# One key block of every three gets its distance factor as the bias of the exponential, and the lists of small work around the attention are re-sorted

## The chip, the cores and the metric

The kernel runs on one core of a Trainium2 chip. The metric is the device time of one execution in microseconds (us). A run of the chip is timed several times and the median is given; one further execution is taken by the hardware profiler, and all durations below come from that one.

## The reference, cut to what matters

Attention over 8 batches, 8 heads, 576 positions and 64 channels, with a window of 128 keys and a penalty that grows with the distance between query and key, is followed by a layer of 8 experts in which every token goes to the one expert with the highest gate.

```python
scores = (1 / np.sqrt(D)) * np.matmul(q, k.transpose(0, 1, 3, 2))
rel = pos[:, None] - pos[None, :]
slopes = 2.0 ** (-8.0 * (np.arange(H) + 1) / H)
mask = (rel >= 0) & (rel < 128)
scores = np.where(mask, scores - slopes * np.abs(rel), -1e9)      # per head
attn = softmax(scores);  x = (attn @ v) as rows of 512            # 4608 tokens
logits = x @ w_gate;  expert = argmax(logits)
y = gate_weight * (relu(x @ w1[expert]) @ w2[expert])             # w1 512x1024, w2 1024x512
```

All of it is float32. A factor that depends on the query alone falls out of the softmax, since it stands above and below the fraction.

## The kernel before, in words

**Attention.** The work is cut into 16 units: 4 pairs of batches (`bp`) times 4 pairs of heads (`hp`). Keys and queries come in 9 blocks of 64 positions (`KB`). A key block meets the queries of its own block and of the next two: block distance 0, where the later keys are masked, 1, where every key is seen, and 2, where the keys that are too old are masked. A unit has four groups `g`: key blocks 0-1, 2-3, 4-5 and 6-8. For a group, `scores(i)` issues 8 or 12 matmuls into a PSUM tile `sp` (two buffers), ScalarE takes the exponential of all 768 columns (L775) into `pe` (six buffers), and VectorE multiplies all 768 columns with the factor `fac`, which holds exp(-slope * distance), zero where masked (L778, L783). `values` multiplies `pe` with the values into the PSUM tile `at` (one buffer of two banks, L804), `finish` copies `at` to `xT` on ScalarE (L821, L823) and sums `pe` over the keys by matmuls (L836); VectorE adds these to `sumT` (L847).

The order of all instructions is written out by hand: the loop runs over `i`, the number of the group, and scores are issued three groups ahead of the values that need them. SyncE loads keys, queries and values two units ahead.

**Small work behind the attention.** When a pair of batches is done, `behind(bp)` hands out a list of small steps, one entry popped by `some()` per group: `gate` (gate logits, matmul and L861), `turn`, `scale_a` to `scale_c` (softmax denominators, argmax; `es` at L952), `count`, `place` (the token's slot in its expert's list), `ones_at` and `enlist` (the lists of token numbers by matmul), and the writing of the token rows to a DRAM tensor `x_rows`. For `bp` 0 the rows are turned on VectorE (`squares_turned`, L1091, into four buffers `xs`), get their scale on POOL (L1099, after `scales_squared` L1073) and leave by POOL's queue, four DMAs for each tile of 128 tokens (`squares_out`, L1108). For `bp` 1 and 2 they are turned on TensorE (L1044) and copied by ScalarE (L1046). The last entry of `bp` 2 is `early_table` and `gather(fixed[0])`: POOL fetches the first 4 x 128 tokens of expert 0 by indirect DMA (L1240).

**Experts.** A group of 512 tokens is gathered, scaled on VectorE (`to_scale`, L1252), turned into columns (`to_columns`: TensorE L1265 and ScalarE L1266 for experts 0 and 1, VectorE L1268 for the others), and multiplied by both weight matrices with seven instead of eight block products: `strassen1` (L1454) and `strassen2` (L1511), fourteen steps each. After each step, `step()` pops one entry of the list `fill`. The small work of the last pair of batches (`with_tail`) fills the 14 steps of expert 0's `strassen1`; the tables of all experts (`table_fixed`, `count_all`, `check_all`, `table_further`, `pieces` L1142), the gather of expert 1 and its preparation fill expert 0's `strassen2`. Before `strassen1`, everything left in `tasks` is issued at once: expert 0's last columns and sums.

## Time and profile before

| | us |
|---|---|
| median of 3 runs (684.91 to 687.83) | 686.86 |
| the profiled execution | 691.06 |
| its span, first to last instruction | 689.2 |
| TensorE matmul busy in the span | 655.8 |
| VectorE / ScalarE / POOL busy in the span | 379.4 / 199.2 / 237.6 |
| unit 1's first value matmul starts at | 21.3 |
| expert 0's first product starts at | 180.7 |
| expert 1's first product starts at | 244.8 |

In the views, PE is TensorE's matmuls, PEld its weight loads, DVE VectorE, ACT ScalarE, SP SyncE; L and a number is a line of the kernel. A group of instructions is shown as engine, operation, output<-inputs, shapes and count, then its busy time and the mean of one. "PEclk" is the granted share of TensorE's clock.

### The profile page before, as it was taken

The page shows a single profiled execution, that of the slowest core. Times are in us where ns is not written, and L with a number is a line of the kernel's source. Part 1 is how long each engine was busy: PE and PEld are TensorE (multiplying, and loading weights), DVE is VectorE, ACT ScalarE, POOL GpSimd, SP SyncE. Part 2 cuts the span into 40 slices and gives each one's busy share as a digit, 9 for nine tenths or more (in the row PEclk, how much of TensorE's full clock was granted, in tenths as well). Part 3 has the DMA queues.
Part 4 walks back from the last instruction along what each step waited for, and adds up shares of the span by engine and source line. Part 5 has one row for each costly group of instructions (what it writes and reads, how often), then busy time and mean ns, then how long its engine had stood idle before and what let it go on. Part 6 is the DMA issues. An engine that isn't in the chain of part 4 may idle for free.

```text
span 689.2 us, 14460 instructions
## 1 busy us (share of the span) xinstructions
PE 655.8 (95%) x6004; PEld 548.2 (80%) x6004; DVE 379.4 (55%) x717; ACT 199.2 (29%) x365; POOL 237.6 (34%) x360
## 2 busy tenths in 40 slices
PE   5899889998999899999999999999999999999996
PEld 4778768687687788878897887888788978878893
DVE  4567769786489476614842564275148435633500
ACT  5555446465331223113202310231131123002210
POOL 8100572215001176117323702652172247023020
PEclk9999899999999999999999999999999999999999
DMA  9677987854516964185448237652844573284010
GB/s 285 200 222 192 287 241 219 289 157 149 165 22 162 386 206 140 57 292 170 155 154 301 57 129 258 212 166 63 296 137 145 178 276 97 86 305 154 1 62 8
DMA packets 63549, 122.00 MB, mean 177 GB/s; under 512 B 5905, under 2 KB 30001, under 8 KB 63474
## 3 DMA queue, kind: packets, MB, share of 16 engines
q1 hardware_dynamic: 51778, 92.78, 42.0%
q0 software_dynamic: 10544, 27.31, 12.4%
q8 instruction: 49, 0.80, 0.5%
q10 hardware_dynamic: 1152, 0.88, 0.4%
q14 instruction: 26, 0.21, 0.1%
HBM read 101.79 MB, written 19.96 MB: 177 GB/s over the span
## 4 chain that ended last, share of the span: by engine, by line
PE 75%; issue 9%; DVE 8%; DMA 4%; POOL 2%; ACT 1%; SPq 0%; POOLq 0%; DVEq 0%; ACTq 0%
PE sp L769 5%; PE at L804 5%; PE pair0b L1511 4%; PE pair0a L1511 4%; PE pair0b L1454 4%; PE pair0a L1454 4%; PE pair1a L1511 4%; PE pair1b L1511 4%; PE pair2b L1454 4%; PE pair1b L1454 4%; PE pair1a L1454 4%; PE pair2a L1454 4%; PE pair2a L1511 4%; PE pair2b L1511 4%; PE m L836 3%
## 5 line engine op out<-in xcount | busy, mean ns | idle before, releaser
L1240 POOL DMA_INDIRECT xg<-x_rows,p_idx x124 | 125.0, 1008 | 37.8 <-issue 37.5
L1534 POOL DMA_INDIRECT out_dram<-zo,s_idx x39 | 44.5, 1140 | 250.6 <-DVE zo L1525 149.6
L769 PE MATMUL sp<-q_sb,k_sb 64*64 64x192 f32 (+2 forms) x1152 | 60.2, 331 | 7.1 <-DMA q_sb<-in_qT_dram 6.9
L775 ACT ACTIVATE pe<-sp 128x768 f32<-128x768 f32 x64 | 51.9, 811 | 49.6 <-PE sp L769 46.7
L804 PE MATMUL at<-pe,v_sb 64*64 64x192 f32 (+2 forms) x1408 | 59.6, 289 | 3.4 <-issue 3.4
L778 DVE TENSOR_TENSOR pe<-pe,fac 128x768 f32<-128x768 f32 x48 | 45.5, 952 | 28.3 <-ACT pe L775 27.8
L804 PEld LDWEIGHTS at<-pe,v_sb 64*64 64x64 f32 x1408 | 48.0, 138 | 9.5 <-issue 6.9
L769 PEld LDWEIGHTS sp<-q_sb,k_sb 64*64 64x64 f32 x1152 | 42.0, 141 | 16.6 <-DMA q_sb<-in_qT_dram 4.3
L1465 ACT ACTIVATE h<-h 128x512 f32<-128x512 f32 x32 | 20.2, 631 | 41.3 <-DVE h L1464 41.3
L836 PE MATMUL m<-pe,ind 128*32 128x192 f32 (+2 forms) x704 | 29.8, 288 | 0.6 <-issue 0.6
L1252 DVE TENSOR_TENSOR xn<-xg 128x512 f32<-128x512 f32 x39 | 26.3, 676 | 3.4 <-DMA xg<-x_rows,g_idx 3.1
L836 PEld LDWEIGHTS m<-pe,ind 128*32 128x32 f32 x704 | 23.2, 110 | 3.0 <-issue 1.0
L1108 POOL DMA_DIRECT2D x_rows<-xs x40 | 21.6, 548 | 6.4 <-POOL xs L1099 1.9
L783 DVE TENSOR_TENSOR pe<-pe,fac 128x768 f32<-128x768 f32 x16 | 15.3, 955 | 15.2 <-ACT pe L775 15.1
L1268 DVE STREAM_TRANSPOSE xgT<-xn 128x512 f32<-128x512 f32 x31 | 22.1, 712 | 1.1
L538 DVE TENSOR_TENSOR w2s<-w 128x512 f32<-128x512 f32 x16 | 10.9, 684 | 19.4 <-DMA w<-in_moe_w_dram 19.4
L1099 POOL COPY xs<-sq 128x16 f32<-128x16 f32 x10 | 2.6, 258 | 53.8 <-ACT sq L1081 53.8
L1566 PE MATMUL pair2a<-w,h 128*128 128x512 f32 x48 | 21.1, 592 | 0.0
L821 ACT COPY xT<-at 128x640 f32<-128x640 f32 (+1 forms) x32 | 18.7, 585 | 6.5 <-PE at L804 4.6
L1454 PE MATMUL pair0b<-xgT,w 128*128 128x256 f32 x72 | 17.2, 382 | 0.0
L1511 PE MATMUL pair1a<-w,h 128*128 128x256 f32 x72 | 17.0, 379 | 0.0
L1454 PE MATMUL pair0a<-xgT,w 128*128 128x256 f32 x72 | 17.0, 379 | 0.0
(375 smaller groups left out, 1393.2 us busy)
## 6 DMA issues: line engine op xcount, KB each, us to landing
w<-in_moe_w_dram SPq DMA_DIRECT2D x29, 2048.0 KB, 7.9
k_sb<-in_kT_dram SPq DMA_DIRECT2D x15, 576.0 KB, 5.6
q_sb<-in_qT_dram SPq DMA_DIRECT2D x15, 576.0 KB, 5.6
v_sb<-in_v_dram SPq DMA_DIRECT2D x30, 288.0 KB, 4.5
x_rows<-xs POOLq DMA_DIRECT2D x16, 264.0 KB, 3.8
x_rows<-xs POOLq DMA_DIRECT2D x32, 66.0 KB, 4.7
x_rows<-xT SPq DMA_DIRECT2D x8, 264.0 KB, 5.2
w<-in_moe_w_dram SPq DMA_DIRECT2D x4, 512.0 KB, 7.7
```

What stands on the lines that cost most here:

```text
L769: nc.tensor.matmul(sp[c * KB : (c + 1) * KB, r, c0 : c0 + n], lhsT=k_sb[u][hs, c, kb * KB : (kb + 1) * KB], rhs=q_sb[u][hs, c, kb * KB : k ...
L775: nc.scalar.activation(pe[:], sp[:, :, :GC], AF.Exp, scale=SCALE)
L778: nc.vector.tensor_tensor(pe.rearrange("p r (k c) -> p r k c", k=2), pe.rearrange("p r (k c) -> p r k c", k=2), fac[:, h0 : h0 + 2, None, ...
L804: nc.tensor.matmul(acc[r * D : (r + 1) * D, c, lo - q0 : hi - q0], lhsT=v_sb[u][c * KB : (c + 1) * KB, kb, r * D : (r + 1) * D], rhs=pe[c ...
L836: nc.tensor.matmul(sm[32 * j : 32 * j + 32, lo - q0 : hi - q0], lhsT=none[:] if pe is None else ind[:, hp, :], rhs=fac[:, 0, :KB] if pe is ...
L1108: eng.dma_start(x_d[r0 : r0 + n * m, a * PW : (a + 1) * PW].rearrange("(k i) w -> i k w", i=TQ), xs[a * TQ : (a + 1) * TQ, p0 // TQ : p0 / ...
L1240: nc.gpsimd.indirect_dma_start(out=to, out_offset=None, in_=where, in_offset=bass.IndirectOffsetOnAxis(ap=idx, axis=0),)
L1252: nc.vector.tensor_tensor(xn[:], x, s.unsqueeze(3).to_broadcast([P, NA, HP, TQ]), op=ALU.mult)
L1268: nc.vector.transpose(to.rearrange("p h (k j) -> p k h j", j=TQ), xn[:])
L1454: nc.tensor.matmul(ps[:, f * 256 : (f + 1) * 256], lhsT=left[m][:, d, fb * P : (fb + 1) * P], rhs=right[m][:, d, :], start=(m in (1, 2, 5) ...
L1511: nc.tensor.matmul(ps[:, :256], lhsT=left[m][:, f, c * P : (c + 1) * P], rhs=right[m][:, f, :], start=(m in (1, 2, 5) and f == 0), stop=Tr ...
L1534: ins = nc.gpsimd.indirect_dma_start(out=out[:, :], out_offset=bass.IndirectOffsetOnAxis(ap=s_idx[:, g["c0"] + j : g["c0"] + j + 1], axis= ...
```

## The change

1. **The exponential and the factor.** Within a group the columns are sorted by block distance: of the three stretches of 128 columns, the first holds distance 0, the second distance 1, the third distance 2 (in the last group, the diagonal block of key block 8 takes a free place in the third). The factor of the query is dropped, since it cancels. What is left of the factor for distance 1 depends on the key alone, that is on the partition: it goes into the exponential as its bias, `mid`, a column of 128 values for each head. So the exponential of a group is three instructions instead of one, 128x512 (distances 0 and 2, both heads) and two of 128x128 with a bias; VectorE multiplies 512 columns instead of 768. The matmuls are as many and as large as before; their moving operand and their output now have up to three stretches of 64 columns. The constants are made in other steps (`seen_i`, `rel_i`, `mid_i`, `far`).
2. **Scores ahead.** In units 0 and 1 the scores are issued two groups ahead, from unit 2 on three as before.
3. **Lists.** `bp` 2: `early_table` is cut in two, the first half (`early_holes`) moves up to the last row writing, the rest and the gather move up by one entry, into the one of `enlist`. The preparation of expert 0 begins one group later, and only its first three entries stay ahead of `strassen1`; the last two of its four column steps and its sums go into the first two steps of `strassen1`. `with_tail` is spread anew: `ones_at`, `enlist` and `end_of_tail` (which loads expert 1's weights) move to `strassen2`'s first six steps, all sums of w2 come into `strassen1`; the eight small row DMAs of the last tile move from SyncE's queue to POOL's. In `strassen2` the tables follow from step 6, expert 1's first two column steps are in steps 11 and 12, and the last two with half of its weight sums and its other sums go into expert 1's `strassen1`.

The diff, cut to its core:

```diff
@@ -641,27 +639,44 @@
-PIECES = ((0, 192), (192, 128), (320, 64))
+seen_i = ac.tile([P, GC], I32, name="seen_i")
 rel_i = ac.tile([P, GC], I32, name="rel_i")
+mid_i = ac.tile([P, 1], I32, name="mid_i")
+NEAR = (0, 1, 4)
 for b in range(2):
-    for c0, n in PIECES:
+    half = slice(b * KB, (b + 1) * KB)
+    nc.gpsimd.iota(seen_i[half, : 5 * KB], pattern=[[0, 5], [1, KB]], base=0, channel_multiplier=-1)
+    for c0, n, e in ((0, 2, 32), (2, 2, 160), (4, 1, 32)):
         nc.gpsimd.iota(
-            rel_i[b * KB : (b + 1) * KB, c0 : c0 + n], pattern=[[1, n]], base=0, channel_multiplier=-1,
-        )
+            rel_i[half, c0 * KB : (c0 + n) * KB], pattern=[[0, n * KB]], base=e, channel_multiplier=-1,
+        )
+    nc.gpsimd.iota(mid_i[half, :], pattern=[[0, 1]], base=-96, channel_multiplier=1)
+seen = ep.tile([P, 2, GC], F32, name="pe")
+far = seen[:, 1, :]
+nc.vector.tensor_copy(seen[:, 0, : 5 * KB], seen_i[:, : 5 * KB])
 rel = ac.tile([P, GC], F32, name="rel")
-nc.vector.tensor_copy(rel[:], rel_i[:])
-far = ep.tile([P, 2, GC], F32, name="pe")
-nc.vector.tensor_scalar(far[:, 0, :], rel[:], scalar1=0.0, scalar2=BIG, op0=ALU.is_lt, op1=ALU.mult)
-nc.vector.tensor_scalar(far[:, 1, :], rel[:], scalar1=127.5, scalar2=BIG, op0=ALU.is_ge, op1=ALU.mult)
-nc.vector.scalar_tensor_tensor(
-    rel[:], in0=rel[:], scalar=0.0, in1=far[:, 0, :], op0=ALU.max, op1=ALU.add,
-)
-nc.vector.tensor_add(rel[:], rel[:], far[:, 1, :])
+nc.vector.tensor_copy(rel[:, : 5 * KB], rel_i[:, : 5 * KB])
+for c0, n, op in ((0, 2, ALU.is_lt), (2, 2, ALU.is_ge), (4, 1, ALU.is_lt)):
+    cs = slice(c0 * KB, (c0 + n) * KB)
+    nc.vector.tensor_scalar(far[:, cs], seen[:, 0, cs], scalar1=0.0, scalar2=BIG, op0=op, op1=ALU.mult)
+nc.vector.tensor_add(rel[:, : 5 * KB], rel[:, : 5 * KB], far[:, : 5 * KB])
 fac = ac.tile([P, H, GC], F32, name="fac")
+mid = ac.tile([P, H], F32, name="mid")
+mid_p = ac.tile([P, 1], F32, name="mid_p")
+nc.vector.tensor_copy(mid_p[:], mid_i[:])
+for h in range(H):
+    nc.vector.tensor_scalar(
+        mid[:, h : h + 1], mid_p[:], scalar1=2.0 ** (-8.0 * (h + 1) / H), scalar2=None, op0=ALU.mult,
+    )
 def factors(hp):
     for h in (2 * hp, 2 * hp + 1):
-        nc.scalar.activation(fac[:, h, :], rel[:], AF.Exp, scale=-(2.0 ** (-8.0 * (h + 1) / H)))
+        nc.scalar.activation(
+            fac[:, h, : 5 * KB], rel[:, : 5 * KB], AF.Exp, scale=-(2.0 ** (-8.0 * (h + 1) / H)),
+        )
 factors(0)
@@ -762,32 +777,40 @@
     sp = ps_s.tile([P, 2, 512], F32, name="sp")
-    for kb, c0, n in GR[g]:
+    for kb in range(2 * g, 2 * g + 2) if g < 3 else range(6, 9):
+        n = min(3, NK - kb)
         for c in range(2):
...
                 nc.tensor.matmul(
-                    sp[c * KB : (c + 1) * KB, r, c0 : c0 + n],
+                    by_distance(sp[c * KB : (c + 1) * KB, r, :GC], kb, 0, n),
                     lhsT=k_sb[u][hs, c, kb * KB : (kb + 1) * KB],
-                    rhs=q_sb[u][hs, c, kb * KB : kb * KB + n], start=True, stop=True,
+                    rhs=q_sb[u][hs, c, kb * KB : (kb + n) * KB].rearrange("p (j x) -> p j x", x=KB),
+                    start=True, stop=True,
                 )
     pe = ep.tile([P, 2, GC], F32, name="pe")
-    nc.scalar.activation(pe[:], sp[:, :, :GC], AF.Exp, scale=SCALE)
     h0 = 2 * units[u][1]
-    if g < 3:
-        nc.vector.tensor_tensor(
-            pe.rearrange("p r (k c) -> p r k c", k=2), pe.rearrange("p r (k c) -> p r k c", k=2),
-            fac[:, h0 : h0 + 2, None, :192].to_broadcast([P, 2, 2, 192]), op=ALU.mult,
-        )
-    else:
-        nc.vector.tensor_tensor(pe[:], pe[:], fac[:, h0 : h0 + 2, :], op=ALU.mult)
+    outer = pe.rearrange("p r (j x) -> p r j x", j=3)[:, :, 0:3:2, :]
+    nc.scalar.activation(
+        outer, sp[:, :, :GC].rearrange("p r (j x) -> p r j x", j=3)[:, :, 0:3:2, :], AF.Exp, scale=SCALE,
+    )
+    w = 2 * KB if g < 3 else 3 * KB
+    nc.vector.tensor_tensor(
+        outer, outer,
+        fac[:, h0 : h0 + 2, : 2 * w].rearrange("p r (j x) -> p r j x", j=2)[:, :, :, : 2 * KB], op=ALU.mult,
+    )
+    for r in range(2):
+        inner = slice(2 * KB, 4 * KB)
+        nc.scalar.activation(
+            pe[:, r, inner], sp[:, r, inner], AF.Exp, bias=mid[:, h0 + r : h0 + r + 1], scale=SCALE,
+        )
     prob[i] = pe
-def block(u, kb):
-    g = min(kb // 2, 3)
-    c0, n = next((c, n) for k, c, n in GR[g] if k == kb)
-    return prob[4 * u + g], c0, n
+def by_distance(x, kb, a, b):
+    if kb == NK - 1:
+        return x[:, 5 * KB :].rearrange("p (j x) -> p j x", j=1)
+    return x.rearrange("p (j k x) -> p j k x", j=3, k=2)[:, a:b, kb % 2, :]
 def values(u, half, kbs):
@@ -797,14 +820,15 @@
     for kb in kbs:
-        pe, c0, n = block(u, kb)
-        lo, hi = max(q0, kb * KB), min(q0 + qn, kb * KB + n)
+        pe = prob[4 * u + min(kb // 2, 3)]
+        lo, hi = max(q0, kb * KB), min(q0 + qn, (kb + 3) * KB)
+        at_kb = (kb, lo // KB - kb, hi // KB - kb)
         for c in range(2):
...
                 nc.tensor.matmul(
-                    acc[r * D : (r + 1) * D, c, lo - q0 : hi - q0],
+                    acc[r * D : (r + 1) * D, c, lo - q0 : hi - q0].rearrange("p (j x) -> p j x", x=KB),
                     lhsT=v_sb[u][c * KB : (c + 1) * KB, kb, r * D : (r + 1) * D],
-                    rhs=pe[c * KB : (c + 1) * KB, r, c0 + lo - kb * KB : c0 + hi - kb * KB],
+                    rhs=by_distance(pe[c * KB : (c + 1) * KB, r, :], *at_kb),
                     start=(c, r) not in begun, stop=True, skip_group_check=True,
...
@@ -1319,16 +1350,19 @@
         rt = [lambda t=t: squares_turned(bp, t) for t in range(TPB)]
-        ro = [lambda t=t: squares_out(bp, t, nc.gpsimd) for t in range(TPB)]
+        ro = [
+            lambda t=t: (squares_scaled(bp, t), squares_out(bp, t, nc.gpsimd)) for t in range(TPB)
+        ]
         return [g3[0:1], g3[1:2], g3[2:] + t3[0:1], t3[1:], a, a2 + rt[0:1], b + rt[1:2], b2 + rt[2:3],
...
     if bp == 1:
-        last = [lambda: squares_turned(0, TPB - 1), lambda: squares_out(0, TPB - 1, nc.gpsimd)]
+        last = [lambda: squares_turned(0, TPB - 1), lambda: squares_scaled(0, TPB - 1),
+                lambda: squares_out(0, TPB - 1, nc.gpsimd)]
         return [g3[0:1] + last, g3[1:2], g3[2:] + t3[0:1], t3[1:], a + rt[0:1], a2 + rt[1:2], b + rt[2:3],
                 b2 + rt[3:4], c + n, [], p + ro[0:2], p2 + ro[2:4] + rs[4:5], o + rs[5:6], o2 + rs[6:7], rs[7:8], e + rs[8:9]]
-    return [g3, t3, a + a2, b + b2 + rt[0:1], c + n + rt[1:2], rt[2:4], p + p2 + ro[0:4], o + o2 + rs[4:6], rs[6:9],
-            e, [early_table, lambda: gather(fixed[0], x_d[: 3 * 2 * S, :])]]
+    return [g3, t3, a + a2, b + b2 + rt[0:1], c + n + rt[1:2], rt[2:4], p + p2 + ro[0:4], o + o2 + rs[4:6],
+            rs[6:9] + [early_holes], e + [early_table, lambda: gather(fixed[0], x_d[: 3 * 2 * S, :])]]
 tasks = []
@@ -1338,9 +1372,14 @@
 NG = 4 * len(units)
-AHEAD = 3
-for i in range(AHEAD):
-    scores(i)
+scored = [0]
+def scores_to(n):
+    while scored[0] < min(n, NG):
+        scores(scored[0])
+        scored[0] += 1
+scores_to(2)
 route_consts()
...
@@ -1364,8 +1403,7 @@
         some()
-    if i + AHEAD < NG:
-        scores(i + AHEAD)
+    scores_to(i + (3 if u < 2 else 4))
     if u in (10, 11):
...
@@ -1379,8 +1417,9 @@
         finish(u, 1)
-    if u == len(units) - 1 and g == 0:
-        tasks.extend(t for _, t in prepare(fixed[0]))
+    if u == len(units) - 1 and g == 1:
+        first = [t for _, t in prepare(fixed[0])]
+        tasks.extend(first[:3])
     if g != 2:
...
@@ -1602,26 +1643,29 @@
     groups[:] = seq
-self_late = []
+after_tail = []
 def with_tail(g, w2s):
...
     rt = [lambda t=t: squares_turned(bp, t) for t in range(TPB)]
-    ro = [lambda: squares_out(bp, 0, nc.sync, 4), lambda: squares_out(bp, 4, nc.sync, 4), lambda: squares_out(bp, 8, nc.sync)]
+    ro = [lambda: squares_out(bp, 0, nc.sync, 4), lambda: squares_out(bp, 4, nc.sync, 4), lambda: squares_out(bp, 8, nc.gpsimd)]
+    o = [lambda: ones_at(bp), lambda: ones_at2(bp)]
+    p = [lambda: place(bp), lambda: place2(bp)]
+    a, a2, b, b2, c, n, q, e = (
+        [lambda f=f: f(bp)]
+        for f in (scale_a, scale_a2, scale_b, scale_b2, scale_c, count, scales_squared, enlist)
+    )
     w = [[f] for f in w2s]
-    a, b, p, o = (
-        [lambda f=f, f2=f2: (f(bp), f2(bp))]
-        for f, f2 in ((scale_a, scale_a2), (scale_b, scale_b2), (place, place2), (ones_at, ones_at2))
-    )
-    c, n, q, e = ([lambda f=f: f(bp)] for f in (scale_c, count, scales_squared, enlist))
     todo = [
-        [lambda k=k: gate(bp, k) for k in range(3)] + rt[0:1], [lambda k=k: turn(bp, k) for k in range(3)] + rt[1:2],
-        a, rt[2:3], b, rt[3:4], c + n, rt[4:5] + w[0], q + p + ro[0:1] + rt[8:9], rt[5:6] + o, rt[6:8] + ro[2:3],
-        ro[1:2] + w[1] + w[2], e + w[3], [table_fixed] + w[4] + w[5],
+        first[3] + [lambda k=k: gate(bp, k) for k in range(3)],
+        first[4] + [lambda k=k: turn(bp, k) for k in range(3)] + first[5] + first[6] + first[7] + first[8],
+        a, a2 + rt[0:1], b, b2 + rt[1:2], c + n + rt[2:3], rt[3:4] + w[0] + w[1],
+        q + p + [lambda: squares_scaled(bp, 0, TPB)], rt[4:5] + rt[8:9] + ro[0:1] + ro[2:3] + w[2],
+        rt[5:8] + ro[1:2], w[3], w[4] + w[5], w[6] + w[7],
     ]
-    self_late.extend(w[6] + w[7])
+    after_tail.extend([o[0:1], o[1:2], [], [], [], e + [end_of_tail]])
     return [(g, t) for t in todo]
@@ -1634,15 +1678,16 @@
         strassen1(g, start=with_tail)
-        end_of_tail()
-        fill.append((g, [lambda: gather(fixed[1], x_d[:, :]), self_late[0]]))
-        fill.append((g, [self_late[1], count_all]))
-        fill.append((g, [check_all]))
-        fill.append((g, [table_further]))
-        fill.append((g, [next_groups, lambda: pieces(slice(NJ, E * NJ), "1")]))
-        fill.append((g, [lambda: pieces(slice(E * NJ, NC), "2")]))
-        fill.extend(prepare(fixed[1]))
+        todo = [t for _, t in prepare(fixed[1])]
+        sums = [f for (f,) in todo[9:]]
+        now = after_tail + [
+            [table_fixed, lambda: gather(fixed[1], x_d[:, :])], [count_all], [check_all], [table_further],
+            [next_groups] + todo[0], todo[1], todo[2] + [lambda: pieces(slice(NJ, E * NJ), "1")],
+            [lambda: pieces(slice(E * NJ, NC), "2")] + sums[0:4],
+        ]
+        fill.extend((g, t) for t in now)
         strassen2(g)
+        fill.extend((None, t) for t in [todo[3] + sums[4:], todo[4], todo[5] + todo[6], todo[7] + todo[8]])
         w_of = lambda k: (w1_a, w2_a) if k % 2 == 0 else (lp["w"], lp["w"])
...
```

## The prediction

> **What bounds the kernel now.** I first read busy time by stage, cutting at the starts of units and experts (columns: length, then busy us and counts of PE, PEld, DVE, ACT, POOL, then PEclk).
>
> ```profile
> 0.00:21.30 21.30, 13.16 (x280) 10.78 (x284) 8.90 (x12) 10.75 (x17) 17.29 (x93) 1.00 0.90 266
> 21.30:64.80 43.50, 41.57 (x1089) 34.99 (x1085) 25.48 (x45) 25.52 (x44) 0.00 (x0) 1.00 0.68 206
> 64.80:96.10 31.30, 25.51 (x544) 20.43 (x533) 25.63 (x53) 12.27 (x21) 17.29 (x36) 0.89 0.92 268
> 96.10:168.90 72.80, 69.36 (x1530) 56.69 (x1534) 56.28 (x134) 43.10 (x75) 24.31 (x52) 0.98 0.67 209
> 168.90:180.70 11.80, 8.66 (x165) 6.94 (x154) 4.53 (x8) 3.81 (x7) 3.67 (x4) 0.86 0.38 99
> 180.70:211.00 30.30, 29.66 (x169) 24.37 (x168) 23.93 (x61) 9.01 (x18) 1.33 (x9) 1.00 0.37 105
> 211.00:244.80 33.80, 30.27 (x149) 26.03 (x148) 23.35 (x65) 6.55 (x14) 7.34 (x7) 0.95 0.83 275
> ```
>
> From 244.8 to 686.6 TensorE is busy 437.65 of 441.8 us; the change leaves that work alone. All that can be won lies before 244.8, and only where PE is idle or slow. Second, PE's list of waits says who holds it up:
>
> ```profile
> PE sp L769 <- DMA q_sb<-in_qT_dram: 6.9, 3, 4.3
> PE at L804 <- issue: 3.4, 3, 1.4
> PE m L1265 <- DVE xn L1252: 3.1, 2, 2.5
> PE m L1142 <- DVE tb L1131: 2.2, 1, 2.2
> PE m L1044 <- DVE sumT L847: 2.0, 2, 1.7
> PE m L856 <- DVE gs L861: 1.8, 2, 1.4
> PE m L1073 <- DVE es L952: 1.7, 1, 1.7
> PE pair1a L1511 <- DVE w2s L539: 1.4, 1, 1.4
> PE m L856 <- DVE sumT L847: 1.1, 1, 1.1
> PE m L967 <- DVE pre L958: 0.8, 1, 0.8
> ```
>
> Eight of the ten wait for VectorE, 14.1 us together, never for the attention's own `pe`: the small work is late because VectorE's queue is full. Third, the same window view at the stretches of half clock:
>
> ```profile
> 71.60:78.40 6.80, 6.69 (x74) 5.66 (x78) 3.66 (x8) 1.56 (x4) 3.73 (x8) 0.50 0.97 284
> 133.00:136.40 3.40, 3.40 (x48) 2.04 (x44) 0.96 (x1) 1.40 (x2) 1.10 (x2) 0.50 0.87 302
> 174.00:177.40 3.40, 3.40 (x50) 2.62 (x44) 1.22 (x3) 1.18 (x2) 0.00 (x0) 0.50 0.36 106
> 228.60:232.00 3.40, 3.40 (x10) 2.69 (x9) 1.39 (x2) 0.00 (x0) 0.00 (x0) 0.50 1.00 358
> ```
>
> Each follows one of those waits (1.7 at 71.5, 1.7 at 132.2, 2.5 at 172.7, 2.2 at 226.6). 17 us at half clock cost another 8.5. Prices come from the groups by shape and from one PE timeline row:
>
> ```profile
> L775 ACT ACTIVATE pe<-sp 128x768 f32<-128x768 f32 x64 | 51.9, 811 | 49.6 <-PE sp L769 46.7 <-ACT xT L823 1.0 <-DMA pace<-pe 0.5
> L778 DVE TENSOR_TENSOR pe<-pe,fac 128x768 f32<-128x768 f32 x48 | 45.5, 952 | 28.3 <-ACT pe L775 27.8 <-DMA v_sb<-in_v_dram 0.3
> L533 DVE TENSOR_TENSOR ws<-w,ws 128x512 f32<-128x512 f32 x16 | 11.0, 690 | 0.0
> 86.93 0.56 PE L1025 MATMUL m<-oc,gsr 128*128 128x96 bf16 x9
> ```
>
> **What the Trainium skill says.** "ScalarE: Activation LUTs", What ACT_TABLE_LOAD costs, prices an activation at 186 ns + 0.833 ns per column, 280 ns where the bias is a column of its own, with 93 ns of overlap back to back. The trace agrees for the first form (0.811 us at 768, 826 stated) and has none of the second. "TensorE: Matmul & The Clock Gate", Part 1, has the clock at half or full, decided on windows of 3.4 us of activity; the stretches above fit (0.50, lengths 3.4 and 6.8). "SBUF — State Buffer", Door 1, warns that PSUM patterns broken below 8 bytes slow matmuls; here stretches are 64 columns, 256 bytes, so I expect nothing, but no run of before shows a stepped float32 output. A stepped moving operand it does show: L1025 reads two stretches of 48; nine matmuls of 0.206 us take 0.56, so 44 ns apart for 96 columns.
>
> **The change, part by part.**
>
> *Multiplication and exponential.* VectorE: 64 x (0.953 - 0.685) = 17 us less (bounds: 0.66 and 0.95). ScalarE: 0.60 (128x512; between 0.586, the 128x512 copies of L1046, and 0.81) plus twice 0.387 - 0.093 = 1.19 against 0.81: +0.38 for a group, +24 us in all (lower bound for one 128x128: the 0.286 of the L823 copies). A plain unit (38.7 to 45.9) has ScalarE at 4.37 of 7.2 us; 4.37 + 1.5 = 5.9 still fits. Behind the longer exponentials are queued the copies of `at` (L821, L823), for which the next unit's values wait; at the unit boundary I count 0.1 to 0.3 us of slack, so I set 0.5 us for 16 units. The latency from scores to `pe` falls: 0.60 plus the larger of 0.69 and 0.59, against 0.81 + 0.95. Matmuls: same number and columns, 0 (bounds below). Constants: ten iotas for six, about 0.7 us later on POOL, but VectorE's chain after them is shorter; covered by the first query load; the `mid` steps (nine of about 0.15) end before the first biased exponential, or delay it by less than 1 us.
>
> *Start (0 to 21.3).* Unit 1's scores wait for its queries until 13.04 (1.9 us). Issued one group later, that wait has the values and sums of unit 0's first half ahead of it, which stand at 13.71 to 15.4 now: **-1.7**.
>
> *64.8 to 96.1.* VectorE has no gap from 58.6 to `es` at 71.3; six multiplications there, 6 x 0.27 = 1.6 of the 1.7 us wait. Then the two half-clock windows (3.4 us) should go, and the 1.1 (eight multiplications since its last gap). The 1.4 before gate's third part stays: VectorE is held there by `squares_turned` of the ninth tile, whose buffer is free only when the fifth tile's DMAs landed, and POOL needs 2.17 + 0.5 us a tile. Counting POOL's five tiles (13.4) and a landing (4.2) from the scales against the faster PE, I get a wait of 3.5, 2.1 more. With even odds of a new half-clock window (0.85): 1.6 + 3.4 + 1.1 - 2.1 - 0.8 = **-3.2**.
>
> *96.1 to 168.9.* 0.5 of the 0.8 wait (L967); all of the 1.7 (L1044: seven multiplications stand in the run that makes it, 1.9) and its window (1.7); ScalarE's extra load delays row copies, for which L1044 waits (0.3 and 0.4 now): +0.8. **-3.1**.
>
> *168.9 to 180.7.* The gather's issue (167.98) comes 3.4 us after POOL's last row DMA and stays tied to those rows; moving its entry up gains little. But its first user stands one group later, behind the 1.6 us of L804 and L836 at 173.3 to 174.9: of 2.5 us some 0.9 stay. The 0.65 before the fourth column step goes, as a product now lies ahead of it, and so should the window (1.7): **-3.9**. The two column steps moved into `strassen1` cost there what they leave here (0.44 to 0.6 each).
>
> *180.7 to 211.* Same matmuls but `enlist` (0.4) gone and two column steps come; sums are ready 2 us before the third product: 0.
>
> *211 to 244.8.* The w2 sums (1.4 wait) end in `strassen1`. The eight small DMAs leave SyncE (5.4 us at 207.4) for POOL (8 x 0.55), side by side, so the last big row DMAs are issued 4 us earlier. The 2.2 before L1142 goes (the tables are spread over more steps), with its window (1.7). New: `enlist` waits for `ones_at`, behind the sums on VectorE, some 0.8 us; expert 1's weights are then loaded 2 us later than at 220.25, needed from 244.8, a landing being 7.9: hidden. The gather moves 2 to 3 us later; at 6.9 us landing its first rows are turned about 0.7 us before PE asks. In expert 1's `strassen1` the moved sums stand just ahead of the third product: 0.4. 1.4 + 2.2 + 1.7 - 0.8 - 0.4, rounded: **-4.0**.
>
> Sum: 1.7 + 3.2 + 3.1 + 3.9 + 4.0 - 0.5 = 15.4, taken as 15. On the profiled execution (span 689.2, 691.06 with what lies around it) that gives 676; that execution is 4.2 above the median of the runs, so on the median 686.86 it gives **672**.
>
> **Rivals.** (1) *The waits only change their releaser*: ScalarE's copies in the dense units (147 to 158: 7.29 + 1.5 of 11.3), POOL's tiles and the two gathers hold PE; half-clock windows stay. The start and half of the rest: 8 us, 679. For it: clock windows need only one gap each, and 1.4 us at 67.0 has no releaser at all. (2) *Slower: the stepped score output.* 1152 score matmuls run four at a time, 288 rounds of 0.324 us. If each of two breaks cost as much as 32 columns (54 ns), a round grows by 0.11, 31 us in all: 703. It decides from 54 ns a round. Against it: L1025 and the 256-byte stretches. (3) *Nothing arrives*, as VectorE keeps 0.95 us on the four-stretch pattern and the tail's new waits eat the list's gain: 686. (4) *All VectorE waits and windows go*, POOL's too: 22 us, 665.
>
> **How the numbers follow.** Forecast 0.61 (own range 667 to 678), rivals 0.20, 0.07, 0.05, 0.07. 672 is the forecast's. The range 663 to 683 holds (4), (1) and the price bounds, leaving out the slower cases. Within 0.5% (3.4 us, about what a measurement of this kernel can tell) lies (3): 0.06; slower 0.07; faster 0.87.
>
> **What would show it.** Right: the multiplication at 0.66 to 0.70 us, VectorE near 362; a group's three exponentials at 0.60, 0.39, 0.39; sp still 0.32 apart a round; no PE wait for `es` over 0.5; the half-clock stretches at 133, 174 and 229 gone; expert 1's first product near 230. Wrong: score matmuls with longer spacing; a PE wait over 2 us for the first gather, or in `strassen2` for `xn`; ScalarE above 90% in a plain unit; expert 1's first product later than 240.

## The result and the profile after

The kernel after takes 682.10 us (median of 9 runs, 679.21 to 683.68), the kernel before beside it 687.83 (9 runs): a ratio of 0.9895, interval 0.9867 to 0.9922, some 7 us less by the ratio and 5.7 by the medians. The forecast was 672, and its range ended at 683. The direction was right; the size was less than half of what was forecast.

The profiled execution of after has a span of 677.5 us and took 679.21 with what lies around it, so on the profiles the change brings 11.7 us (689.2 to 677.5), against 15.4 in the sum of the prediction. The window view of after, cut at the same events as the windows of before (columns: length, then busy us and counts of PE, PEld, DVE, ACT, POOL, then PEclk, DMA share and GB/s):

```profile
0.00:18.54 18.54, 12.45 (x257) 10.43 (x261) 6.33 (x21) 11.31 (x28) 15.45 (x97) 1.00 0.95 266
18.54:64.01 45.47, 42.37 (x1105) 35.53 (x1096) 22.44 (x48) 32.31 (x87) 0.00 (x0) 1.00 0.79 216
64.01:95.38 31.37, 24.43 (x544) 18.85 (x536) 22.36 (x51) 15.30 (x41) 17.55 (x37) 0.95 0.97 277
95.38:164.60 69.22, 67.65 (x1526) 55.78 (x1530) 50.19 (x134) 50.45 (x127) 24.71 (x52) 1.00 0.68 214
164.60:172.23 7.63, 5.88 (x156) 4.96 (x149) 3.50 (x6) 3.62 (x8) 3.23 (x4) 1.00 0.51 143
172.23:202.71 30.48, 30.19 (x166) 24.96 (x167) 23.61 (x61) 10.19 (x21) 4.89 (x16) 1.00 0.37 107
202.71:230.85 28.14, 28.01 (x150) 24.41 (x149) 19.94 (x57) 5.14 (x13) 8.21 (x9) 1.00 0.85 276
230.85:295.14 64.29, 63.75 (x315) 53.29 (x315) 40.79 (x67) 12.93 (x25) 26.23 (x25) 1.00 0.56 194
```

The first number after each pair of cuts is what to compare. Line by line the lengths were 21.30, 43.50, 31.30, 72.80, 11.80, 30.30 and 33.80 in before. Five lines went the way of the sum (the sixth was to stay as it was). The third did not: 31.37 us, as long as before, where 3.2 less was forecast. The second grew by 2.0. The last line is expert 1 up to the first product of the next expert; it took 62.5 in before, and the 1.8 more are column steps of expert 1 that were moved into it and a wait of 0.5.

PE's list of waits in after (us in total, times, longest):

```profile
PE sp L785 <- DMA q_sb<-in_qT_dram: 5.4, 2, 4.4
PE at L828 <- issue: 3.3, 3, 1.2
PE m L859 <- issue: 2.7, 2, 2.0
PE m L879 <- DVE gs L884: 1.6, 1, 1.6
PE sp L785 <- issue: 1.6, 2, 1.3
PE m L1296 <- DVE xn L1283: 1.1, 1, 1.1
PE m L1096 <- DVE es L975: 0.7, 1, 0.7
PE pair2a L1495 <- DVE xs L539: 0.5, 1, 0.5
```

The waits for VectorE that were to go are gone or short: `es` 0.7 instead of 1.7, the first gather's `xn` 1.1 instead of 3.1, the tables (2.2) and the w2 sums (1.4) not in the list at all. What is new stands under "issue", PE's gaps for which the profile has no releaser: 7.6 us in the three lines, 4.2 in before. The prices were right (page of after; busy us, then mean ns):

```profile
L798 DVE TENSOR_TENSOR pe<-pe,fac 128x512 f32<-128x512 f32 x64 | 43.8, 687 | 45.7 <-ACT pe L794 44.9
L785 PE MATMUL sp<-q_sb,k_sb 64*64 64x192 f32 (+2 forms) x1152 | 58.9, 324 | 6.9 <-DMA q_sb<-in_qT_dram 5.4
L794 ACT ACTIVATE pe<-sp 128x512 f32<-128x512 f32 x64 | 38.2, 598 | 37.9 <-issue 15.9
L804 ACT ACTIVATE pe<-sp,mid 128x128 f32<-128x128 f32 x128 | 39.7, 366 | 0.0
```

Sixteen score matmuls at full clock (start, us), in before and in after:

```profile
81.04 0.83 PE L769 MATMUL sp<-q_sb,k_sb 64*64 64x192 f32 x16
72.59 0.83 PE L785 MATMUL sp<-q_sb,k_sb 64*64 64x192 f32 x16
```

The multiplication takes 0.687 (0.685 forecast), the exponentials 0.598 and 0.366 (0.60 and 0.39). The sixteen score matmuls take 0.83 us in both kernels, so the rival of the stepped output is out. (The means on the pages, 0.324 and 0.331, mix shapes and clocks.)

Of the prediction's signs of being right all came but one: VectorE is at 363.9 (362 forecast), the half-clock stretches at 133, 174 and 229 are gone, expert 1 starts at 230.9; only PE's wait for `es`, 0.7, is above the 0.5 that was named. None of the signs of being wrong came. All of them were looked for in a single execution, and they did not tell 672 from 682.

One thing must be known for the experiments: in three of their four series the kernel before itself took 726 to 731 us (in the third 687.6, on the same chip as in the second), because TensorE stands still in the experts there and then runs at half clock, and what ends its standing still the profile does not name; the ratios of those series say little, and they are read by the stages before expert 1.

### The profile page after: what moved, and what is told of

It is laid out like the page before. It is cut to its first block, busy times and chain, and to the rows that moved or that the text cites. A ratio compares the mean times of both kernels' runs of the same rounds, so it can differ in the third digit from the quotient of the medians.

```text
span 677.5 us, 14654 instructions
## 1 busy us (share of the span) xinstructions
PE 649.8 (96%) x6004; PEld 543.5 (80%) x6004; DVE 363.9 (54%) x727; ACT 217.0 (32%) x493; POOL 240.3 (35%) x372
## 4 chain that ended last, share of the span: by engine, by line
PE 57%; issue 25%; POOL 10%; DMA 4%; DVE 2%; ACT 1%; POOLq 0%; DVEq 0%; ACTq 0%
PE pair1a L1552 4%; PE pair1b L1552 4%; PE pair0b L1495 4%; PE pair0a L1495 4%; PE pair0a L1552 4%; PE pair0b L1552 4%; PE pair2b L1495 4%; PE pair2a L1495 4%; POOL xg L1271 4%; DMA x_rows<-xs 3%; PE pair1b L1495 3%; PE pair1a L1495 3%; PE pair2a L1552 3%; PE pair2b L1552 3%; PE pair0a L1607 2%
## 5 line engine op out<-in xcount | busy, mean ns | idle before, releaser
L798 DVE TENSOR_TENSOR pe<-pe,fac 128x512 f32<-128x512 f32 x64 | 43.8, 687 | 45.7 <-ACT pe L794 44.9
L794 ACT ACTIVATE pe<-sp 128x512 f32<-128x512 f32 x64 | 38.2, 598 | 37.9 <-issue 15.9
L804 ACT ACTIVATE pe<-sp,mid 128x128 f32<-128x128 f32 x128 | 39.7, 366 | 0.0
L1137 POOL DMA_DIRECT2D x_rows<-xs x48 | 26.0, 549 | 9.5 <-DMA x_rows<-xs 4.6
L538 DVE TENSOR_TENSOR w2s<-w 128x512 f32<-128x512 f32 x16 | 10.9, 684 | 20.8 <-DMA w<-in_moe_w_dram 20.8
L1607 PE MATMUL pair2a<-w,h 128*128 128x512 f32 x48 | 21.1, 592 | 0.0
L1495 PE MATMUL pair0a<-xgT,w 128*128 128x256 f32 x72 | 17.1, 380 | 0.7 <-ACT xgT L1297 0.7
L1495 PE MATMUL pair0b<-xgT,w 128*128 128x256 f32 x72 | 17.2, 382 | 0.0
L1552 PE MATMUL pair1a<-w,h 128*128 128x256 f32 x72 | 17.1, 380 | 0.0
```

The lines of the kernel that those rows point to most:

```text
L794: nc.scalar.activation(outer, sp[:, :, :GC].rearrange("p r (j x) -> p r j x", j=3)[:, :, 0:3:2, :], AF.Exp, scale=SCALE,)
L798: nc.vector.tensor_tensor(outer, outer, fac[:, h0 : h0 + 2, : 2 * w].rearrange("p r (j x) -> p r j x", j=2)[:, :, :, : 2 * KB], op=ALU.mult,)
L804: nc.scalar.activation(pe[:, r, inner], sp[:, r, inner], AF.Exp, bias=mid[:, h0 + r : h0 + r + 1], scale=SCALE,)
L1495: nc.tensor.matmul(ps[:, f * 256 : (f + 1) * 256], lhsT=left[m][:, d, fb * P : (fb + 1) * P], rhs=right[m][:, d, :], start=(m in (1, 2, 5) ...
L1552: nc.tensor.matmul(ps[:, :256], lhsT=left[m][:, f, c * P : (c + 1) * P], rhs=right[m][:, f, :], start=(m in (1, 2, 5) and f == 0), stop=Tr ...
L1607: nc.tensor.matmul(ps[:], lhsT=g["h"][:, fb, :], rhs=g["w2"][:, fb, :], start=(fb == 0), stop=(fb == FB - 1),)
```

## The experiments

The table has, for each profile, the lengths between starts of units (a unit starts with its first matmul of values), up to expert 0's and expert 1's first product, in us, and the ratio to before in the same series. Series 1 is e1 to e4, series 2 e5 to e8, series 3 e9 to e12, series 4 e13 and x1 to x3. The interval of a ratio is 0.2 to 0.6% to either side, 1.5 to 4 us.

| kernel | unit 0 starts | units 0, 1 | units 2 to 5 | unit 6 starts | 6 to 9 | 9 to 15 | 15 to expert 0 | expert 1 starts | ratio to before |
|---|---|---|---|---|---|---|---|---|---|
| before | 10.3 | 19.7 | 34.7 | 64.8 | 37.4 | 66.7 | 11.8 | 244.8 | |
| e1 before | 10.0 | 19.3 | 33.9 | 63.2 | 37.9 | 65.2 | 11.7 | 242.2 | 0.9995 (0.9966 to 1.0023) |
| e9 before, 6 buffers | 10.5 | 19.6 | 33.3 | 63.4 | 36.0 | 65.2 | 10.3 | 239.0 | 0.9977 (0.9956 to 0.9998) |
| e2 exponential only | 10.9 | 19.9 | 35.6 | 66.4 | 40.7 | 63.1 | 12.2 | 246.5 | 1.0043 (1.0004 to 1.0082) |
| e6 the same | 10.3 | 19.1 | 35.2 | 64.6 | 38.5 | 63.1 | 12.0 | 242.3 | 1.0080 (1.0046 to 1.0114) |
| e3 order only | 8.3 | 17.4 | 35.2 | 61.0 | 38.1 | 65.0 | 9.6 | 232.3 | 1.0049 (1.0023 to 1.0076) |
| e7 the same | 8.6 | 18.4 | 35.0 | 62.0 | 41.0 | 65.1 | 8.7 | 235.3 | 0.9981 (0.9944 to 1.0017) |
| e10 order, 6 buffers | 9.0 | 16.3 | 35.6 | 60.8 | 36.3 | 65.0 | 8.2 | 228.9 | 0.9849 (0.9798 to 0.9900) |
| e13 the same | 9.1 | 18.5 | 35.2 | 62.9 | 33.9 | 65.5 | 10.3 | 231.1 | 0.9983 (0.9952 to 1.0014) |
| after | 9.5 | 19.1 | 35.4 | 64.0 | 37.6 | 63.0 | 7.6 | 230.9 | 0.9895 (0.9867 to 0.9922) |
| e5 after | 9.2 | 21.1 | 34.8 | 65.2 | 39.3 | 63.2 | 13.0 | 239.2 | 1.0009 (0.9979 to 1.0039) |
| e4 after, 6 buffers | 9.2 | 19.3 | 38.1 | 66.6 | 32.7 | 63.3 | 9.9 | 231.1 | 1.0004 (0.9978 to 1.0030) |
| e8 the same | 9.5 | 19.1 | 37.6 | 66.2 | 34.3 | 63.9 | 13.0 | 236.0 | 0.9926 (0.9892 to 0.9961) |
| e12 the same | 9.1 | 20.1 | 34.7 | 63.9 | 36.3 | 63.3 | 7.8 | 229.9 | 0.9838 (0.9786 to 0.9890) |
| e11 e12, copies on VectorE | 9.2 | 19.2 | 35.7 | 64.1 | 35.6 | 63.0 | 7.8 | 229.2 | 0.9846 (0.9790 to 0.9901) |
| x1 columns only | 8.5 | 18.8 | 33.6 | 60.9 | 37.1 | 65.3 | 8.7 | 230.7 | 1.0001 (0.9972 to 1.0029) |
| x2 three exponentials | 9.3 | 18.8 | 36.2 | 64.3 | 37.1 | 66.2 | 8.8 | 235.1 | 1.0106 (1.0067 to 1.0144) |
| x3 hybrid | 9.1 | 20.1 | 33.8 | 63.0 | 36.9 | 64.2 | 10.2 | 233.0 | 1.0013 (0.9987 to 1.0040) |

**The same kernels again (e1, e5).** Unchanged kernels.

> The kernel before itself, unchanged, to see how far one profiled execution stands from the others. The profiled executions differ by 11.7 us of span (689.2 to 677.5), the medians by about 6 and the paired ratio says 7.2. Theory A, the profile of before was an unlucky one: its four windows at half clock (8.5 us) are not in most runs; then most runs here show a mean clock of 0.988 or more where the profiled one had 0.985, and spans near 686; a new profile shows two or three windows, not four. Theory B, before always has these windows and it is the profile of after that was lucky: clocks here stay at 0.985 and spans at 688 to 690.

> The kernel after itself once more, beside before on the same chip. On the chip of the first four runs before took 726.7 us instead of 687.8, and the versions with the new lists reached the first product of expert 1 about 10 us earlier (232.3 and 231.1 against 242.2) but stood still for 8 to 11 us at 250 us, so that nothing arrived at the end. Theory A: on a chip where before takes 687 to 688 the gain up to expert 1's first product is 10 to 14 us and 2 to 4 of it are lost behind it, 7 us at the end (681). Theory B, the profiled 11.7 us is the usual gain and the slower runs are chance: 676 to 678.

Measured: windows at half clock before expert 1 stand at 71, 170 and 225 us in e1, and at 21, 72 and 222 in e9 (before with more buffers). The profile of before had four stretches: those at 72 and 229 come back in both, the one at 133 in neither, the one at 174 in e1 alone. In the series with e9, 27 runs of before lie between 684.7 and 693.7 us (clock 0.982 to 0.992), median 687.6: the execution that the prediction was built on, 691.06, is among the slower quarter. That of after, 679.21, is the fastest of its nine. So theory A of e1 holds in part: both profiles were off, to opposite sides. e5 met TensorE's standing still; the first line of its waits shows it, and after brought nothing there, so neither theory of e5 could be told at the end of the run:

```profile
PE pair1a L1495 <- DVE h L1517: 9.2, 1, 9.2
```

**The row buffers (e4, e8, e12, e9).** In 64 to 96 us the rows of the first pair of batches are turned by VectorE into `xs` and written out by POOL. The timelines of VectorE and POOL in after (start, us, operation, idle time before it and its releaser):

```profile
81.04 0.70 DVE L1118 STREAM_TRANSPOSE xs<-xT 128x512 f32<-128x512 f32 x1
82.76 0.71 DVE L1118 STREAM_TRANSPOSE xs<-xT 128x512 f32<-128x512 f32 x1 [1.02 <-POOL xs L1126]
83.40 1.25 DVE L798 TENSOR_TENSOR pe<-pe,fac 128x512 f32<-128x512 f32 x2
87.88 0.71 DVE L1118 STREAM_TRANSPOSE xs<-xT 128x512 f32<-128x512 f32 x1 [1.33 <-DMA x_rows<-xs]
...
93.44 0.71 DVE L1118 STREAM_TRANSPOSE xs<-xT 128x512 f32<-128x512 f32 x1 [2.39 <-DMA x_rows<-xs]
94.08 0.65 DVE L798 TENSOR_TENSOR pe<-pe,fac 128x512 f32<-128x512 f32 x1
94.64 0.68 DVE L884 TENSOR_TENSOR gs<-m,sumT 128x512 f32<-128x512 f32 x1
```

```profile
74.25 2.17 POOL L1137 DMA_DIRECT2D x_rows<-xs  x4 [0.29 <-POOL xs L1126]
76.41 0.21 POOL L1126 COPY xs<-sq 128x16 f32<-128x16 f32 x1
78.81 0.55 POOL L1137 DMA_DIRECT2D x_rows<-xs  x1 [2.20 <-DMA x_rows<-xs]
```

POOL's ninth row DMA starts at 78.81, 0.59 us behind the landing of the first (78.22), its 17th at 85.44, 0.59 behind that of the ninth (84.85): each waits for the landing of the eighth before it. VectorE's turns wait for POOL and the DMAs, and behind each turn stand a multiplication or a gate sum, for one of which PE waits (1.58 before L879). The edit gives the first pair of batches six buffers:

```
+        rows_2 = pool(att, "rows_2", 2)
+        ints = ep.tile([P, 2, GC], I32, name="pe")   # in place of the integer constant tiles
...
+        own = rows_2 if bp == 0 and t in (4, 5) else rows
+        xs_of[bp, t] = own.tile([P, NA, PW], F32, name="xs")
```

> After, with six instead of four buffers for the rows of the first image pair that VectorE turns and POOL writes out (two more buffers in a pool of the attention's own; the two integer constant tiles lie in a buffer of the probabilities to make room). Theory A: in 64 to 102 us of after PE waits 1.98 us (L859, at 83.04) and 1.58 us (L879, at 93.80) behind VectorE's turns, which wait for a row buffer that POOL's DMAs free late, and a window at half clock follows (1.7); with two buffers more these go and the stretch from unit 6 to unit 9 shrinks from 37.6 to 33 to 34 us: 3 to 4 us less than after, 678 to 679 against 682. Theory B, the limit is POOL's eight outstanding DMAs and not the buffers: PE's waits stay in this stretch under other names, and the time stays within 1 us of after.

> The same kernel as in e4 (after, with two more row buffers for the first image pair), now beside after on one chip. In e4 the stretch from unit 6 to unit 9 took 32.7 us, where after's profile has 37.6. Theory A: 3 to 5 us less than after at expert 1's first product, and 2 to 4 at the end. Theory B: later waits (the gather of expert 0 behind POOL's last rows, loads) take it back before the end: within 1 us of after.

> After with two more row buffers once more (the kernel of e4 and e8), as the measure for e10 and e11 in the same call. Unit 6 to unit 9 at 33 to 34 us, as in the two profiles before (32.7 and 34.3); 0.5 to 1% faster than before at the end if PE's stand at 250 us is short on this chip, and the same as before if it is 8 us or more.

> Before with the two more row buffers of e4 and e8. In before VectorE's turns of the rows wait once for a buffer (PE's 1.44 us for L856 at 94.65), in after three times. Theory A, the shorter multiplication made the row buffers the limit of this stretch: here the stretch from unit 6 to unit 9 falls by 1 to 3 us only (from 37.4 and 37.9 in two profiles), against 4.9 in after. Theory B, the buffers held before as much: it falls by 4 to 5 us as well.

Measured: unit 6 to 9 takes 32.7, 34.3 and 36.3 us where after took 37.6 and 39.3; in before 36.0 against 37.4 and 37.9. The turns of e12 no longer wait:

```profile
82.16 1.30 DVE L1120 STREAM_TRANSPOSE xs<-xT 128x512 f32<-128x512 f32 x2
...
87.73 1.30 DVE L1120 STREAM_TRANSPOSE xs<-xT 128x512 f32<-128x512 f32 x2
...
90.63 0.70 DVE L1120 STREAM_TRANSPOSE xs<-xT 128x512 f32<-128x512 f32 x1
```

What PE waits for in this stretch of e12 (us in total, times, longest):

```profile
PE at L829 <- issue: 4.7, 2, 2.9
PE m L860 <- issue: 1.4, 1, 1.4
```

The lengths hold windows at half clock, which come and go (two in before and e1, one in after, e8 and e9, none in e4 and e12), so PE's idle time says more. What the buffers do is clear: PE waited 1.4 to 4.8 us for `gs` in this stretch in all eight profiles with four buffers, and 0 to 0.4 in all ten with six. PE's idle time fell from 7.0 and 7.6 us (after, e5) to 3.8 and 4.2 (e4, e8; e11 has 4.2), and theory A of e4 holds there. In e12 it did not fall: 7.0 us, of which 6.6 are gaps without a releaser, and its 36.3 us missed the 33 to 34 expected; its length is below after's by no more than the one window at half clock that after has. POOL itself became no faster: in e12, too, its 17th DMA waits 1.97 us, until 0.59 behind the landing of the ninth. So theory B of e4 names what sets POOL's pace, but with six buffers VectorE and PE no longer feel it.

In the second series e8 is at 0.9926 and after at 1.0009, 6 us apart by the medians; in the third, e12 takes 677.61 us against 687.59, 0.9838. In before the same buffers bring 0.2% and PE's idle time stays (5.8 and 6.1 us to 5.8), so the 1.4 to 1.9 us of e9 are a window at half clock. Theory A of e9 has the number, but its cause, the shorter multiplication, is not it: the order with the old multiplication gains as much from the buffers (PE idle 6.1 and 7.6 us in e3 and e7, 4.7 and 3.8 in e10 and e13). It is the new order that made them the limit.

**Which half carries it (e2, e6; e3, e7; e10, e13).** The change's diff was divided below `finish`: constants, `scores`, `values` and `finish` are the exponential's part, all behind them the order's. e10 and e13 are the order's part with the six buffers.

```
 e2, e6 (and nothing behind finish):
-            nc.scalar.activation(pe[:], sp[:, :, :GC], AF.Exp, scale=SCALE)
+            nc.scalar.activation(outer, ..., AF.Exp, scale=SCALE)
...
+                    pe[:, r, inner], sp[:, r, inner], AF.Exp, bias=mid[:, h0 + r : h0 + r + 1], scale=SCALE,
 e3, e7 (and nothing ahead of it):
-            if i + AHEAD < NG:
-                scores(i + AHEAD)
+            scores_to(i + (3 if u < 2 else 4))
...
```

> Before, with only the exponentials, the multiplication and the columns by block distance of the change; the old lists and three groups of scores ahead. Theory A (the sum of the prediction by stages, but without the gain in 64.8 to 96.1 us, which the row writes of POOL take): VectorE's relief is worth 3 to 4 us between 96 and 169 us, less 0.5 to 1 for ScalarE's longer groups: about 3 us less than before, 684 to 685 against 687.5. Theory B, ScalarE's longer exponentials cost as much as VectorE's relief brings: 687 to 688, and the change's whole gain is in the lists.

> The same kernel as in e2 (exponentials, multiplication and columns of the change, lists of before), in one call with after and the order alone. On the other chip it was 0.4% slower than before and its first product of expert 1 came at 246.5 against 242.2, with a wait of 3.4 us for gate's sums (L879) at 93 us and two windows at half clock behind it. Theory A: VectorE's relief is eaten by POOL's row writes, so that it is within 3 us of before on any chip. Theory B: it was that chip; here it is 3 to 4 us faster, as the prediction's parts for 96 to 169 us say.

> Before, with only the order of work and the lists of the change; exponential, multiplication and columns stay as before. Theory A: the three parts of the sum that come from the lists (1.4 at the start, 4.2 at 168.9 to 180.7, 4.0 at 211 to 245) arrive without the new exponential, but the first needs VectorE free in the dense units: 6 to 8 us less than before, 680 to 682. Theory B: the lists need the room that the shorter multiplication makes, so that alone they bring under 3 us: 685 to 687.

> The same kernel as in e3 (the lists and the order of work of the change, exponential and multiplication of before). Theory A: the lists carry the gain: the first product of expert 1 comes 9 to 10 us earlier than in before, as on the other chip, and the end 5 to 7 us earlier (681 to 683), so that after adds only 0 to 2 us to it. Theory B: without the shorter multiplication the lists bring half: 684 to 685.

> The order and lists of the change with two more row buffers, but the exponential and multiplication of before. Beside after with the same buffers (e12) it isolates the multiplication's worth where row buffers no longer limit. Theory A: VectorE's 17 us less are worth 1 to 2 us in unit 6 to 9 (the wait for es, 2.6 in the profiles with the old multiplication) and 2 us in unit 9 to 15 (65.0 against 63.1 so far), but the new form loses 3 to 4 us before unit 6 (order alone reached unit 6 at 61.0 and 62.0, the four profiles of the new form with it at 64.0 to 66.6): this kernel is within 1 us of e12 at expert 1's first product. Theory B: the multiplication's relief is worth over 3 us in all.

> The kernel of e10 (order and lists of the change, six row buffers, exponential and multiplication of before), as the measure for the next three. Unit 6 at 60.5 to 62 us, 1.3 to 1.6% faster than before where before takes 687.

Measured: the exponential's part alone is not faster than before. It reaches expert 1 at 246.5 and 242.3, where before has 244.8 and 242.2; its ratios, 0.4% and 0.8% slower, come from the two disturbed series. That is theory B of e2. The order alone reaches expert 1 at 232.3 and 235.3, 7 to 10 us ahead of e1: theory A of e3, up to there; at the end nothing of it arrived in these series. In the second series after (1.0009) is not ahead of the order alone (0.9981). In the third, where nothing blurs the end, e10 has 678.46 us (0.9849) and e12 677.61 (0.9838): with or without the new exponential and multiplication, the time is the same within the intervals. By stage, e12 against e10: unit 6 starts 3.1 us later, unit 9 to 15 takes 1.7 less, 15 to expert 0 0.4 less. Theory A of e10 holds. e13 is the kernel of e10 once more and starts unit 6 at 62.9, not at 60.8: two executions of one kernel can be 2 us apart there.

**Where the new exponential loses (e11, x1, x2, x3).** The seven profiles with three exponentials a group on the new order (after, e4, e5, e8, e11, e12, x2) start unit 6 at 63.9 to 66.6; the five with one (e3, e7, e10, e13, x1) at 60.8 to 62.9. That is 64.9 and 61.5 on the means; 0.7 of the 3.4 us between them are a window at half clock in e4, e5 and e8 each, if such a window of 3.4 us costs 1.7. e11 takes the `xT` copies off ScalarE in units 0 to 2:

```
-            nc.scalar.copy(xT...)
+            copy = nc.vector.tensor_copy if u < 3 else nc.scalar.copy
+            copy(xT...)
```

> After with two more row buffers (e12), and the copies of the values' sums to xT (L845, L847: 0.6, 0.5 and 0.3 us a unit half) in units 0 to 2 on VectorE instead of ScalarE. Theory A: before unit 6 the new form loses 3 to 4 us against the order alone, because ScalarE, with the factors of the next heads and three exponentials a group, is busy 7.0 to 7.1 us of 9 in units 0 and 1 and its copies stand behind exponentials; with 1.5 us a unit taken off, unit 6 starts 2 to 3 us earlier than in e12 (at 62 to 64). Theory B: the loss is in PE's own gaps without a releaser (16.3, 21.9 and 32.9 us in after), which follow a 16 KB packet of the instruction queue by 0.2 to 0.5 us: unit 6 starts where it starts in e12.

Unit 6 starts at 64.1, as in e12 (63.9): theory A falls. The windows of units 0, 1 and 2, first e7 (order alone), then e11 (ACT is the fourth busy time):

```profile
8.60:17.20 8.60, 7.65 (x218) 6.90 (x212) 4.80 (x5) 6.21 (x12) 7.74 (x53) 1.00 1.08 310
17.20:27.00 9.80, 8.78 (x232) 7.58 (x227) 4.86 (x7) 5.93 (x10) 2.11 (x9) 1.00 0.86 225
27.00:35.20 8.20, 7.94 (x225) 7.10 (x220) 5.18 (x8) 5.08 (x9) 0.00 (x0) 1.00 0.93 245
```

```profile
9.20:19.10 9.90, 7.71 (x216) 7.03 (x212) 4.52 (x8) 6.01 (x17) 7.81 (x59) 1.00 1.08 286
19.10:28.40 9.30, 8.23 (x234) 7.49 (x230) 4.89 (x9) 5.38 (x15) 0.00 (x0) 1.00 0.77 203
28.40:36.70 8.30, 7.88 (x225) 6.60 (x217) 5.37 (x10) 5.75 (x17) 0.00 (x0) 1.00 0.90 240
```

ScalarE's busy time is about that of the order alone (17.1 against 17.2 us in the three units; 20.5 in e12), and the start of unit 6 is not. x1 keeps the columns and takes back the three exponentials; x2 has them without the columns; x3 has one exponential in units 0 to 3 and in each last group, the biased ones elsewhere:

```
 x1:  exp(pe[:], sp[:, :, :GC]);  pe = pe * fac            (all 768 columns, by distance)
 x2:  exp(pe[:, :, :256]);  exp(pe[:, r, 256:384], bias=nil) for r = 0, 1;  pe = pe * fac
 x3:  if u < HP or g == 3: as x1   else: as after
```

> e13 with the columns by block distance on TensorE, but one exponential of 128x768 and a multiplication of all 768 columns (no bias; in each unit's last group the multiplication is two, of 640 and 128). Theory A, TensorE's stepped outputs and inputs make PE's own gaps in the first units: unit 6 starts at 64 or later, as in after. Theory B, it is ScalarE's three exponentials: unit 6 starts at 60.5 to 62 as in e13, and the end is within 1 us of e13.

> e13 with three exponentials a group (128x512, and twice 128x128 with a bias of zeros) in place of one of 128x768; columns and multiplication as before. Theory B, the longer work of ScalarE makes the loss: unit 6 starts at 64 or later (the multiplication waits 0.4 us longer for its input, so it can be more than in after). Theory A, the columns: unit 6 starts at 61 to 62.5.

> e12 (after with six row buffers), but in units 0 to 3 and in every unit's last group the one exponential and the full multiplication of x1; the biased form in the other groups from unit 4 on. If theory B holds, it has the order's early unit 6 (61 to 62.5) and most of the shorter multiplication's 1.7 us between unit 9 and unit 15: 1 to 3 us less than e13. If theory A holds, unit 6 starts at 64 and it ends where e12 does, within 1 us of e13.

Measured: x1 starts unit 6 at 60.9, x2 at 64.3. The columns cost nothing; x2, with three exponentials in place of one, is 1.4 us behind the latest of the five and 1.0106 where e13 in the same series is 0.9983. Theory B holds as far as it names the exponentials: two to three us before unit 6. By what path is not settled. That ScalarE is too busy, e11 speaks against, for the three units that it changes. PE's waits up to unit 6, first x1, then x2, show where the time is lost:

```profile
PE sp L776 <- DMA q_sb<-in_qT_dram: 5.1, 3, 4.3
PE sp L776 <- issue: 1.7, 2, 1.2
...
PE m L844 <- issue: 0.2, 1, 0.2
```

```profile
PE sp L773 <- DMA q_sb<-in_qT_dram: 5.2, 2, 4.2
PE sp L773 <- issue: 1.4, 2, 0.7
PE m L846 <- issue: 1.0, 1, 1.0
PE at L814 <- issue: 0.6, 1, 0.6
```

Waits for queries and gaps without a releaser come to 5.8 to 7.1 us in the five profiles and to 8.0 to 9.3 in the seven. A score buffer is read by three instructions that take 1.1 us together (0.49 from the first to the second, 0.62 for the pair) instead of one of 0.81, and of these buffers there are two; but in none of the twelve does PE wait for ScalarE to leave one. This is theory B of e11 as far as the place goes; why three exponentials should widen PE's own gaps no run shows. x3 was no earlier than e13 (63.0 and 62.9) and not ahead at the end (1.0013): both gains were not had together.

## Why the prediction was wrong in size

By its own steps, on the profiled executions (measured as differences of the windows above):

| step | forecast | measured |
|---|---|---|
| start and first units, with ScalarE's slack of 0.5 | -1.2 | -0.8 (to unit 6) |
| 64.8 to 96.1 | -3.2 | +0.1 |
| 96.1 to 168.9 | -3.1 | -3.6 |
| 168.9 to 180.7 | -3.9 | -4.2 |
| 180.7 to 211 | 0 | +0.2 |
| 211 to 244.8 | -4.0 | -5.7, of which 1.8 came back in expert 1: -3.9 |
| tail behind the last matmul | 0 | +0.5 |
| sum | -15.4 | -11.7 |

**The order's steps were right.** The gather's user one group later, the w2 sums and tables spread over more steps, the eight small DMAs on POOL: 168.9 to 180.7 and 211 to 244.8 came out within 0.3 us, and -5.7 stands in all thirteen profiles with the new order (28.1 or 28.2 us from expert 0's second layer to expert 1, 33.8 or 33.9 without). That -5.7 net of 1.8 is the forecast -4.0 is luck in part: the column steps that went over to expert 1 were not in the sum of this stretch. The stretch from 168.9 is less sure: with the new order it took 7.6 to 13.0 us, 9.5 on the mean of thirteen, where the five profiles with the old order have 11.6; the longest (e5, e8) have two windows at half clock at 168 to 179 us. So after's -4.2 is the best case; on the means it is 2 us. Rival 1, that waits only change their releaser, was right in one stretch alone.

**The step that failed first is 64.8 to 96.1.** The prediction saw the chain of POOL's tiles and counted one wait of 3.5 us at gate. From POOL's first scaling to VectorE's ninth turn it took 13.4 us for five tiles and 4.2 for a landing, 17.6; the chain took 19.9 us in before (73.98 to 93.89) and 22.5 in after (70.95 to 93.44), because POOL also waits, tile for tile, for earlier DMAs to land (2.2 us at 76.6), and VectorE meets it three times (1.0 to 2.4 us). POOL started 3.0 us earlier and VectorE's ninth turn came 0.5 earlier. In front of that turn PE's waits for VectorE were exchanged for gaps without a releaser (1.4 us in before, 4.1 in after), a term that the sum left as it was without a reason. One of the two half-clock windows did go (6.8 us in before, 3.4 in after); that both would go was not sure either: e5, e8 and e11, with the new multiplication, have windows between 70 and 78 us again. With six buffers the wait at gate is gone, and PE's idle time in units 6 to 9 is some 3 us less in three of the four profiles (not in e12).

**The second is ScalarE's slack, "0.5 us for 16 units".** It was read from a plain unit's busy share, 4.37 + 1.5 of 7.2. The order alone brings unit 6 to 60.8 to 62.9, where three profiles of before have 63.2 to 64.8: 2.3 us on the means (x1 counted with the order), 1.7 forecast. Three exponentials take two to three us away again. The price itself was right: from the Trainium skill, "ScalarE: Activation LUTs", What ACT_TABLE_LOAD costs (280 ns and 0.833 a column), the estimate is 387 ns for 128 biased columns, and after has 366; the term was put at 0.5 from ScalarE's room, and the loss came up in PE's own gaps.

**VectorE's relief was overrated.** The sum gave it 1.6, 3.4, 1.1, 0.5, 1.7 and 1.7, 10 us in all. It is real from unit 9 to 15: 63.0 to 63.9 us against 65.0 to 65.5 with the new order and the old multiplication, where PE's waits for `sumT` and `pre` shrink (2.0 and 0.8 in e10, 0.8 and 0.4 in e12). That is 2 us. The wait for `es` was 0 to 2.2 us in the six profiles of the new form and 0 to 2.7 in the five with one exponential, so after's 0.7 is no proof. What the exponential loses takes the 2 us back: nothing is left in e12 against e10. The list of waits named VectorE eight times, but those for the tables and the w2 sums (3.6 us) are gone with the order alone (e10), the first gather's fell there from 3.1 to 1.6, and that for `gs` went with the buffers: most of it was cured by giving the same work another place.

**One sum of the rivals was wrong.** The stepped output was priced at 288 rounds of 0.324 us. That is 93 us, more than the 60.2 for which PE is busy with these matmuls; 0.324 is how long one takes, and in both traces rounds of four start 0.163 us apart. By the rival's own rule the breaks would have cost some 16 us, not 31.

**The last is the step from the profile to the median.** The prediction took the profiled execution of before as 4.2 us above the median and expected the same of after. Measured, 3.2 above (691.06 to 687.83) and 2.9 below (679.21 to 682.10): 6 of the 11.8 us between these two executions lie in which ones were profiled. Windows at half clock that another execution need not have (133 in neither e1 nor e9, 174 in one of them) had been counted as gains in full. Of the 10 us between 672 and 682, 3 come from the stages and 7 from this step, the largest single error of the forecast. That the execution of before would be slow and that of after fast against their own medians could not be known from one profile; that a single one need not stand for the median could.
